# Decode attention behind a full DMA stream: an uneven load of wq, transposes of 32 keys, and V as the stationary operand in the last two tiles

## The chip, the cores and the metric

The kernel runs on one core of a Trainium2 chip. The metric is the device time of one execution in microseconds. Every run listed here is fast, so all comparisons are fast against fast. A run's time is about 1.7 to 2.0 us longer than the span of its profile (for example 1288.89 us against 1287.1 us in the profiled execution of the kernel before). Times inside a run, such as "1282.67 us", are counted from the start of the span.

## The reference

One decode step: layer norm, attention of one query per head over a cache of 8192 keys, a SwiGLU block beside it, and the residual.

```python
# B=4, D=512, H=32, Sk=8192, Dh=128, F=1792, everything bfloat16
xn = layernorm(x)
q  = (xn @ wq).reshape(B, 1, H, Dh).transpose(0, 2, 1, 3)
p  = softmax(einsum("bhqd,bhkd->bhqk", q, k_cache) * Dh ** -0.5)
o  = einsum("bhqk,bhkd->bhqd", p, v_cache).transpose(0, 2, 1, 3).reshape(B, 1, H * Dh)
out = x + o @ wo + (silu(xn @ w_gate) * (xn @ w_up)) @ w_down
```

K and V are 256 MiB each; with the weights 550.77 MB have to be read.

## The kernel before

The cache is cut into 64 tiles of two heads and one batch, 4 MB of K and 4 MB of V each. SP (SyncE) issues all the large loads in program order; a pool of five 4 MB slots holds K tiles, V tiles and weights. VectorE transposes K in SBUF, 16 keys per partition at a time, PE multiplies, and two tiles share one softmax. V is two tiles behind K (`LP = 2`).

```python
NT, T, TG, NTG, NV, LP = 64, 128, 16, 8, 4, 2      # tiles, rows per partition, rows per piece, pieces ...

wq_t = slot()                                       # one transfer, 128 partitions x 32 KB
nc.sync.dma_start(out=wq_t[:], in_=A_wq.rearrange("(p c) n -> p (c n)", c=EC))

def t_piece(n, g):                                  # VectorE: 16 keys per partition at once
    ...
    nc.vector.transpose(out=kt..., in_=src...)
def s_piece(n, g):                                  # PE: four score matmuls of 512 columns on that piece
    ...
def pt_turn(gr):                                    # VectorE: transposes the probabilities of two tiles into ptz
    ...
def pv_chunk(n, k):                                 # V is the moving operand: 32 matmuls of 512 columns a tile
    mm(o_acc[j % 2][...], pt[n // 2][...], v_tiles[n][:, k * 512:(k + 1) * 512], start=(k == 0))
def pv_last(xps, ts):                               # V is the stationary operand: 128 matmuls of 2 columns a tile
    ...
def fin_1(j):                                       # o_acc -> SBUF and a sum over its four parts
    nc.scalar.copy(out=o_sb..., in_=o_acc[j % 2][:])            # ScalarE
    nc.vector.tensor_tensor(out=o_sb[:], in0=o_sb[:], ...)      # VectorE, waits for the copy
    nc.vector.reduce_sum(out=o1[:], in_=o_sb...)                # VectorE

for i in range(NT + LP):
    # load_k(i + 2); load_v(i), the last two V tiles in 4 and 5 pieces; weights of the FFN, wo (at i = 57)
    if i < NT:
        for g in range(NTG):
            t_piece(i, g); s_piece(i, g)
            if g == 0 and bb == 0 and gr > 0: pt_turn(gr - 1)
        ...
    elif i == NT:
        pt_turn(NT // 2 - 1)                        # probabilities of tiles 62 and 63
    npv = i - LP                                    # the V tile of this turn
    if npv == NT - 1:                               # tile 63
        pv_last(xps, range(T // 2)); fin_2(...); pv_last(xps, range(T // 2, T)); fin_3(...)
    elif npv >= 0:
        for k in range(NK): pv_chunk(npv, k) ...
        if bv == B - 1 or npv == NT - 2: fin_1(jv)  # after every fourth tile, and after tile 62
        ...
```

Of the kernel before, what the change touches and what calls it, by code (L numbers as in the profile page):

```python
# [8 lines left out]
dt = mybir.dt  # L9
ACT = mybir.ActivationFunctionType  # L10
ALU = mybir.AluOpType
# [4 lines left out]
def kernel(  # L16
# [13 lines left out]
    nc = tc.nc  # L30
    P = nc.NUM_PARTITIONS

    B, Sq, D = A_x.shape
    _, H, Sk, Dh = A_k_cache.shape
# [3 lines left out]
    EC = D // P  # L38
    FC = F // P
    M = B * H  # L40
    HT = 2
    NT = M // HT
    T = HT * Sk // P
    QB = 32
    NQ = P // QB
    TG = 16
    NTG = T // TG
    NV = 512 // Dh
    SLOT = T * Dh
    NSLOT = 5  # L50
# [11 lines left out]
    slots = ctx.enter_context(tc.tile_pool(name="slots", bufs=NSLOT))  # L62
    const = ctx.enter_context(tc.tile_pool(name="const", bufs=1))
    persist = ctx.enter_context(tc.tile_pool(name="persist", bufs=1))
    kt_pool = ctx.enter_context(tc.tile_pool(name="ktp", bufs=5))
    pp = ctx.enter_context(tc.tile_pool(name="pp", bufs=2))
    small = ctx.enter_context(tc.tile_pool(name="small", bufs=2))
    psS = ctx.enter_context(tc.tile_pool(name="psS", bufs=2, space=bass.MemoryType.PSUM))
# [6 lines left out]
    def mm(out_ap, lhsT, rhs, start, **kw):  # L75
        nc.tensor.matmul(out_ap, lhsT=lhsT, rhs=rhs, start=start, stop=True,  # L76
                         skip_group_check=True, **kw)

    def slot():
        return slots.tile([P, SLOT], dt.bfloat16, name="slot")  # L80
# [3 lines left out]

    x_sb = persist.tile([B, D], dt.bfloat16, name="x_sb")
    nc.scalar.dma_start(out=x_sb[:], in_=x_flat[:, :])
    wq_t = slot()
    nc.sync.dma_start(out=wq_t[:], in_=A_wq.rearrange("(p c) n -> p (c n)", c=EC))

    k_tiles, v_tiles = {}, {}  # L90

# [6 lines left out]
    def load_v(n, parts=(T,)):  # L98
        j, b = divmod(n, B)
        t_ = slot()  # L100
        src = A_v_cache[b, j * HT:(j + 1) * HT, :, :].rearrange("h (p t) d -> (h p) (t d)", t=T)
        c0 = 0
        for w in parts:
            c1 = c0 + w * Dh
            nc.sync.dma_start(out=t_[:, c0:c1], in_=src[:, c0:c1])
            c0 = c1
        v_tiles[n] = t_
# [11 lines left out]
    zq = [const.tile([P, 2, 4, ZW], dt.bfloat16, name=f"zq{i}") for i in range(2)]  # L119
    for z_ in zq:  # L120
        nc.gpsimd.memset(z_[:], 0.0)
    xnt_w = const.tile([P, EC, QB], dt.bfloat16, name="xnt_w")
    nc.gpsimd.memset(xnt_w[:], 0.0)
    o_acc = [psO.tile([P, 512], dt.float32, name=f"oacc{i}") for i in range(2)]
    for o_ in o_acc:
# [35 lines left out]
    nc.scalar.activation(out=std[:], in_=vsum[:], func=ACT.Sqrt, bias=epst[:, 0:1], scale=1.0 / D)  # L161
    rstd = persist.tile([B, 1], dt.float32, name="rstd")
    nc.vector.reciprocal(out=rstd[:], in_=std[:])
    xn_bf = kt_pool.tile([B, D], dt.bfloat16, name="kt")
    nc.vector.tensor_scalar(out=xn_bf[:], in0=xc[:], scalar1=rstd[:, 0:1], scalar2=None, op0=ALU.mult)  # L165


    xnt_ps = psX.tile([P, EC, B], dt.bfloat16, name="xps")
    for c in range(EC):
        nc.tensor.transpose(xnt_ps[:, c, :], xn_bf[0:B, c:D:EC], ident[0:B, 0:B])  # L170
    nc.vector.tensor_copy(out=xnt_w[:, :, 0:B], in_=xnt_ps[:])


    NH = H * Dh // 512 // NQ
    q_ps = [psS.tile([P, 512], dt.float32, name="sps") for _ in range(NH)]
    for c in range(EC):
        for half in range(NH):
            for cg in range(NQ):
                n0 = c * H * Dh + (half * NQ + cg) * 512
                mm(q_ps[half][cg * QB:(cg + 1) * QB, :], xnt_w[:, c, :], wq_t[:, n0:n0 + 512], start=(c == 0))  # L180

    q_bf = slots.tile([P, NH, 2, 8, NQ, QB], dt.bfloat16, name="slot")
    for half in range(NH):
        for par in range(2):
            src = q_ps[half][:].rearrange("p (x i r) -> p x i r", x=8, r=2)[:, :, :, par]
# [83 lines left out]
                out=zq[gr % 2][a * QB:(a + 1) * QB, :, :, XO + a * QB].rearrange("p b (j r) -> p r j b", r=2),  # L269
                in_=qt[a * QB:(a + 1) * QB, half, :, hh * 2:hh * 2 + 2, cg * B + bp * 2:cg * B + bp * 2 + 2])  # L270

    def t_piece(n, g):

        w = TG * Dh
        kt = kt_pool.tile([P, w], dt.bfloat16, name="kt")
        src = k_tiles[n][:, g * w:(g + 1) * w].bitcast(dt.uint32)
        nc.vector.transpose(out=kt[:].bitcast(dt.uint32).rearrange("p (j t r) -> p t j r", j=2, r=QB),  # L277
                            in_=src.rearrange("p (t j r) -> p t j r", j=2, r=QB))
        kts[n, g] = kt

    def s_piece(n, g):
        gr, bb = divmod(n, 2)
        if bb == 0 and g == 0:
            s_ps[gr] = psS.tile([P, 512], dt.float32, name="sps")
        kt = kts.pop((n, g))[:].rearrange("p (j n r) -> p j n r", j=2, r=2)
        off = XO - 2 * (bb * NTG + g)
        for jp in range(4):
            mm(s_ps[gr][:], zq[gr % 2][:, bb, jp, off:off + P], kt[:, jp // 2, :, jp % 2],
               start=(bb == 0 and g == 0 and jp == 0))
# [6 lines left out]
    def max_2(gr):  # L296

        mps = psM.tile([P, 512], dt.float32, name="mps")
        nc.tensor.matmul(mps[:, 0:P], lhsT=nmx.pop(gr)[:, 0:1].to_broadcast([P, P]), rhs=ident_f[:, :],  # L299
                         is_transpose=True, start=True, stop=True, skip_group_check=True)  # L300
        nm = small.tile([P, HT, 2], dt.float32, name="nm")
        nc.vector.tensor_reduce(out=nm[:], in_=by_row(mps[:, 0:P]), axis=AX.XY, op=ALU.max, negate=True)  # L302
        nc.vector.tensor_tensor(out=nm[:], in0=nm[:], in1=rowb_q[:], op=ALU.mult)
        nb = small.tile([P, 1], dt.float32, name="nb")
        nc.vector.reduce_sum(out=nb[:], in_=nm[:], axis=AX.XY)
        p_ = pp.tile([P, 512], dt.bfloat16, name="p_")
        rs = small.tile([P, 1], dt.float32, name="rs")
        nc.scalar.activation(out=p_[:], in_=s_ps.pop(gr)[:], func=ACT.Exp, bias=nb[:, 0:1], scale=qscale,
                             accum_out=rs[:])
        pt[gr] = p_  # L310
        rs_t[gr] = (rs, mps)
# [27 lines left out]
        mm(o_acc[j % 2][b * QB:b * QB + w, :], pt[n // 2][:, off:off + (w - 1) * QB + 1:QB],  # L339
           v_tiles[n][:, k * 512:(k + 1) * 512], start=(k == 0))  # L340

    def pv_last(xps, ts):

        n = NT - 1
        for t in ts:
            k, u = divmod(t, NV)
            off = p_off(n, k) + u * QB
            mm(xps[:, :, B - 1], v_tiles[n][:, t * Dh:(t + 1) * Dh], pt[n // 2][:, off:off + NV * QB + 1:NV * QB],
               start=(t == 0))

    def fin_1(j):
        o_sb = pp.tile([P, NV, Dh], dt.float32, name="o_sb")
        nc.scalar.copy(out=o_sb[:].rearrange("p u d -> p (u d)"), in_=o_acc[j % 2][:])  # L353
        nc.vector.tensor_tensor(out=o_sb[:], in0=o_sb[:], in1=rowu[:].unsqueeze(2).to_broadcast([P, NV, Dh]), op=ALU.mult)  # L354
        o1 = pp.tile([P, Dh], dt.float32, name="o1")
        nc.vector.reduce_sum(out=o1[:], in_=o_sb[:].rearrange("p u d -> p d u"), axis=AX.X)  # L356
        osb[j] = o1
# [4 lines left out]
    def fin_2(j, xps, nb=B, start=True):  # L362
        mm(xps[:, :, 0:nb], osb.pop(j)[:], rowy[:, :, 0:nb], start=start)
# [25 lines left out]
    for i in range(NT + LP):  # L389

        if i + 2 < NT:
            load_k(i + 2)
        nv = i + 2 - LP
        if 0 <= nv < NT:
            load_v(nv, (32, 32, 32, 16, 16) if nv == NT - 1 else (32,) * 4 if nv == NT - 2 else (T,))
        if i == R_FFN - 3:
            load_ffn()
        if i == R_FFN:
            do_ffn()
        if i == R_WO - 2:  # L400
            load_wo()
        gr, bb = divmod(i, 2)
        if i < NT:
            for g in range(NTG):
                t_piece(i, g)
                s_piece(i, g)
                if g == 0 and bb == 0 and gr > 0:
                    pt_turn(gr - 1)
            if bb == 1:
                if gr + 1 < NT // 2:  # L410
                    build_q(gr + 1)
                max_1(gr)
        elif i == NT:
            pt_turn(NT // 2 - 1)
        npv = i - LP
        if npv == NT - 1:
            xps = x_tile()
            pv_last(xps, range(T // 2))
            fin_2(H // HT - 1, xps, nb=B - 1, start=False)
            pv_last(xps, range(T // 2, T))  # L420
            fin_3(H // HT - 1, xps)
            wo_ready = H
        elif npv >= 0:
            for k in range(NK):
                pv_chunk(npv, k)
                if k == 4 and i < NT and bb == 1:
                    max_2(gr)
            jv, bv = divmod(npv, B)
            if bv % 2 == 0:
                row_sums(npv // 2)  # L430
            if bv == B - 1 or npv == NT - 2:
                fin_1(jv)
            if bv == B - 1:
                if jv < JL:
                    fin_q(jv)
                    if jv % 2 == 1:
                        wo_ready = (jv + 1) * HT
                else:
                    xps = x_tile()
                    fin_2(jv, xps)  # L440
                    fin_3(jv, xps)
                    wo_ready = (jv + 1) * HT
        elif i < NT and bb == 1:
            max_2(gr)
        if i >= R_WO:
            for _ in range(8):
                if wo_next < wo_ready:
                    wo_mm(wo_next)
                    wo_next += 1
# [40 lines left out]
```

## Time and profile before

| | |
|---|---|
| median of three runs | 1288.78 us (1288.62 to 1288.79) |
| span, mean granted TensorE clock of the profiled run | 1287.1 us, 0.933 |
| data | 550.77 MB, 428 GB/s over the span |
| the last piece of V lands | 1282.67 us |
| the last matmul on V ends | 1283.30 us |
| after it | normalisation, four matmuls with wo, two casts, output: 3.8 us |

The main lines of the page and of the tail are shown and read in the prediction below.

### The profile page before, as it was taken

The page shows a single profiled execution, that of the slowest core. Times are in us where ns is not written, and L with a number is a line of the kernel's source. Part 1 is how long each engine was busy: PE and PEld are TensorE (multiplying, and loading weights), DVE is VectorE, ACT ScalarE, POOL GpSimd, SP SyncE. Part 2 cuts the span into 40 slices and gives each one's busy share as a digit, 9 for nine tenths or more (in the row PEclk, how much of TensorE's full clock was granted, in tenths as well). Part 3 has the DMA queues.
Part 4 walks back from the last instruction along what each step waited for, and adds up shares of the span by engine and source line. Part 5 has one row for each costly group of instructions (what it writes and reads, how often), then busy time and mean ns, then how long its engine had stood idle before and what let it go on. Part 6 is the DMA issues. An engine that isn't in the chain of part 4 may idle for free.

```text
span 1287.1 us, 11189 instructions
## 1 busy us (share of the span) xinstructions
PE 1083.1 (84%) x4778; PEld 430.3 (33%) x4778; DVE 738.1 (57%) x951; ACT 39.7 (3%) x87; POOL 5.3 (0%) x13
## 2 busy tenths in 40 slices
PE   4888888888888798897997888888887988978788
PEld 1334333333333333332333333333333333333334
DVE  6663556546556556466556566465465465573544
ACT  1000000000000000000000000000000000000000
POOL 1000000000000000000000000000000000000000
PEclk9898898998989999898998989989899898989899
DMA  9999999999999999999999999999999999999997
GB/s 407 427 430 435 437 425 437 429 436 431 432 435 428 436 432 433 431 432 435 431 435 428 434 432 431 436 431 433 430 434 431 437 430 432 433 431 427 433 434 304
DMA packets 21529, 551.49 MB, mean 428 GB/s; under 512 B 2268, under 2 KB 2792, under 8 KB 3944
## 3 DMA queue, kind: packets, MB, share of 16 engines
q1 hardware_dynamic: 21464, 550.78, 99.4%
q8 instruction: 37, 0.61, 0.2%
q14 instruction: 12, 0.10, 0.0%
q10 hardware_dynamic: 16, 0.01, 0.0%
HBM read 550.77 MB, written 0.00 MB: 428 GB/s over the span
## 4 chain that ended last, share of the span: by engine, by line
DMA 50%; PE 31%; DVE 14%; issue 5%; ACT 1%; SPq 0%; DVEq 0%
DMA slot<-in_A_k_cache_dram 44%; PE oacc L76 17%; PE sps L76 12%; DVE kt L277 11%; DMA slot<-in_A_v_cache_dram 6%; PE mps L76 1%; DVE ptz L318 1%; DVE o L356 1%; PE xps L76 1%; DVE o_sb L354 1%; ACT o_sb L353 0%; PE mps L299 0%; DVE otn L377 0%; PE yo_ps L76 0%; DVE rcp L328 0%
## 5 line engine op out<-in xcount | busy, mean ns | idle before, releaser
L76 PE MATMUL sps<-kt,zq 128*128 128x512 bf16 x2048 | 578.3, 421 | 145.2 <-DVE kt L277 128.7
L277 DVE STREAM_TRANSPOSE kt<-slot 128x1024 uint32<-128x1024 uint32 x512 | 587.6, 1210 | 90.4 <-DMA slot<-in_A_k_cache_dram 89.5
L76 PE MATMUL oacc<-slot,ptz 128*8 128x512 bf16 x2016 | 450.4, 379 | 0.4 <-DMA slot<-in_A_v_cache_dram 0.4
L76 PEld LDWEIGHTS <-zq 128*128 128x128 bf16 x2048 | 212.0, 104 | 496.1 <-issue 317.0
L76 PEld LDWEIGHTS <-ptz 128*8 128x8 bf16 x2016 | 177.5, 92 | 258.1 <-issue 27.8
L328 DVE RECIPROCAL rcp<-mps 128x4 f32<-128x4 f32 x32 | 5.9, 183 | 281.9 <-PE mps L76 281.9
L354 DVE TENSOR_TENSOR o_sb<-o_sb,rowu 128x512 f32<-128x512 f32 x16 | 11.1, 693 | 89.2 <-ACT o_sb L353 89.0
L76 PE MATMUL xps<-rowy,o 128*32 128x4 f32 (+1 forms) x228 | 13.5, 205 | 37.3 <-DVE o L356 37.3
L293 DVE TENSOR_REDUCE mx<-sps 128x1 f32<-128x512 f32 x32 | 22.1, 692 | 18.5 <-PE sps L76 18.5
L76 PEld LDWEIGHTS xps<-rowy,o 128*32 128x32 f32 (+1 forms) x228 | 12.1, 154 | 44.9 <-DVE o L356 44.9
L268 DVE COPY zq<-qt 32x8 bf16<-32x8 bf16 x128 | 21.3, 166 | 1.3
L302 DVE TENSOR_REDUCE nm<-mps 128x4 f32<-128x64 f32 x32 | 7.2, 225 | 24.0 <-PE mps L299 24.0
L356 DVE TENSOR_REDUCE o<-o_sb 128x128 f32<-128x512 f32 x16 | 16.3, 1020 | 0.5
L76 PEld LDWEIGHTS mps<-rowb,rs 128*128 128x128 f32 x64 | 9.5, 186 | 13.8 <-issue 13.8
L76 PEld LDWEIGHTS <-slot 128*128 128x128 bf16 x272 | 11.7, 126 | 3.5 <-DVE slot L188 2.6
L76 PE MATMUL mps<-rowb,rs 128*128 128x4 f32 x64 | 12.3, 263 | 0.0
L353 ACT COPY o_sb<-oacc 128x512 f32<-128x512 f32 x16 | 9.4, 586 | 76.8 <-PE oacc L76 76.8
L377 DVE TENSOR_TENSOR otn<-xps,rcp 32x16 bf16<-32x16 f32 x28 | 4.8, 170 | 11.7 <-PE xps L76 10.3
L299 PE MATMUL mps<-ident_f,mx 128*128 128x128 f32 x32 | 10.3, 323 | 0.8 <-DVE mx L293 0.8
L299 PEld LDWEIGHTS mps<-ident_f,mx 128*128 128x128 f32 x32 | 4.3, 133 | 14.7 <-DVE mx L293 14.2
L170 PE MATMUL xps<-ident,kt 4*128 4x4 bf16 x4 | 0.3, 173 | 10.1 <-DVE kt L165 10.1
L76 PE MATMUL yo_ps<-slot,otn 128*4 128x256 bf16 x64 | 8.2, 281 | 0.3 <-DVE otn L366 0.3
(150 smaller groups left out, 148.5 us busy)
## 6 DMA issues: line engine op xcount, KB each, us to landing
slot<-in_A_k_cache_dram SPq DMA_DIRECT2D x64, 4096.0 KB, 39.2
slot<-in_A_v_cache_dram SPq DMA_DIRECT2D x62, 4096.0 KB, 36.8
slot<-in_A_v_cache_dram SPq DMA_DIRECT2D x7, 1024.0 KB, 22.3
slot<-in_A_wq_dram SPq DMA_DIRECT2D x1, 4096.0 KB, 12.3
slot<-in_A_wo_dram SPq DMA_DIRECT2D x1, 3584.0 KB, 40.2
slot<-in_B_w_gate_dram SPq DMA_DIRECT2D x1, 1792.0 KB, 31.9
slot<-in_B_w_up_dram SPq DMA_DIRECT2D x1, 1792.0 KB, 35.8
slot<-in_B_w_down_dram SPq DMA_DIRECT2D x1, 1792.0 KB, 30.9
```

Source lines behind the costliest of these rows:

```text
L76: nc.tensor.matmul(out_ap, lhsT=lhsT, rhs=rhs, start=start, stop=True, skip_group_check=True, **kw)
L268: nc.vector.tensor_copy(out=zq[gr % 2][a * QB:(a + 1) * QB, :, :, XO + a * QB].rearrange("p b (j r) -> p r j b", r=2), in_=qt[a * QB:(a + ...
L277: nc.vector.transpose(out=kt[:].bitcast(dt.uint32).rearrange("p (j t r) -> p t j r", j=2, r=QB), in_=src.rearrange("p (t j r) -> p t j r", ...
L293: nc.vector.reduce_max(out=mx[:], in_=s_ps[gr][:], axis=AX.X)
L299: nc.tensor.matmul(mps[:, 0:P], lhsT=nmx.pop(gr)[:, 0:1].to_broadcast([P, P]), rhs=ident_f[:, :], is_transpose=True, start=True, stop=True ...
L302: nc.vector.tensor_reduce(out=nm[:], in_=by_row(mps[:, 0:P]), axis=AX.XY, op=ALU.max, negate=True)
L318: nc.vector.transpose(out=t_[y * HP:(y + 1) * HP, :, y, :, :].rearrange("p s u x -> p s (u x)"), in_=p_[y * HP:(y + 1) * HP, :].rearrange( ...
L328: nc.vector.reciprocal(out=rcp[j][:, :, 2 * bp:2 * bp + 2], in_=mps[:, P:P + B].rearrange("p (y b) -> p y b", y=HT))
L353: nc.scalar.copy(out=o_sb[:].rearrange("p u d -> p (u d)"), in_=o_acc[j % 2][:])
L354: nc.vector.tensor_tensor(out=o_sb[:], in0=o_sb[:], in1=rowu[:].unsqueeze(2).to_broadcast([P, NV, Dh]), op=ALU.mult)
L356: nc.vector.reduce_sum(out=o1[:], in_=o_sb[:].rearrange("p u d -> p d u"), axis=AX.X)
L377: nc.vector.tensor_tensor(out=otn[q0:q1, blk * 4:blk * 4 + 4, :], in0=xps[q0:q1], in1=r_[q0:q1, y, :].unsqueeze(1).to_broadcast([QB, 4, B] ...
```

## The change

Its intent can be read from the diff. One group of the DMA engines finishes the stream later than the rest (nine of the sixteen, 5.87 to 7.84 us behind the fastest at the last piece of V in the kernel before), since it also carries the fetches of instructions (37 packets on q8 and 12 on q14). The change (1) gives eight of the engines more of wq, so that the other eight start K earlier (the eight are called the lower ones here), (2) halves the number of transposes, for fewer instructions on VectorE and so fewer fetches, and (3) shortens PE's work at the end: tile 62 joins tile 63 in having V stationary, and the last piece of V has 8 rows instead of 16. The diff, cut to its core:

```diff
-    wq_t = slot()
-    nc.sync.dma_start(out=wq_t[:], in_=A_wq.rearrange("(p c) n -> p (c n)", c=EC))
+    wq_t, wq_u = slot(), slot()
+    nc.sync.dma_start(out=wq_t[:, 0:C1 * NQ_], in_=A_wq[0:C1 * P, :].rearrange("(p c) n -> p (c n)", c=C1))
+    for g in range(PH // QB):
+        r0 = C1 * P + g * 2 * QB
+        nc.sync.dma_start(out=wq_u[g * QB:(g + 1) * QB, 0:2 * NQ_],
+                          in_=A_wq[r0:r0 + 2 * QB, :].rearrange("(r e c) n -> e r (c n)", r=4, e=8))
...   # the projection of q reads five blocks of wq in place of four
-    kt_pool = ctx.enter_context(tc.tile_pool(name="ktp", bufs=5))
+    kt_pool = ctx.enter_context(tc.tile_pool(name="ktp", bufs=3))        # buffers of twice the size
...
-            load_v(nv, (32, 32, 32, 16, 16) if nv == NT - 1 else (32,) * 4 if nv == NT - 2 else (T,))
+            load_v(nv, (64, 32, 16, 8, 8) if nv == NT - 1 else (64, 64) if nv == NT - 2 else (T,))
...
-            for g in range(NTG):
-                t_piece(i, g)
-                s_piece(i, g)
-                if g == 0 and bb == 0 and gr > 0:
+            nd = 1 if i >= NT - 2 else ND                                # ND = 2
+            for k in range(0, NTG, nd):
+                t_piece(i, k, nd)
+                for g in range(k, k + nd):
+                    s_piece(i, g)
+                if k == 0 and bb == 0 and gr > 0:
                     pt_turn(gr - 1)
...
-        if npv == NT - 1:
+        if npv == NT - 2:
             xps = x_tile()
-            pv_last(xps, range(T // 2))
-            fin_2(H // HT - 1, xps, nb=B - 1, start=False)
-            pv_last(xps, range(T // 2, T))
+            pv_last(npv, xps, range(T), start=True)
+            row_sums(npv // 2)
+            fin_2(H // HT - 1, xps, nb=B - 2, start=False)
+        elif npv == NT - 1:
+            pv_last(npv, xps, range(T))
             fin_3(H // HT - 1, xps)
...
-            if bv == B - 1 or npv == NT - 2:
+            if bv == B - 1 or npv == NT - 3:
                 fin_1(jv)
```

Not shown above: the probabilities `p_` and the copy `o_sb` get one buffer instead of two.

More of the change, by code (lines that the diff above doesn't have):

```diff
@@ L47 @@
     NTG = T // TG
+    ND = 2
     NV = 512 // Dh
@@ L86 @@
     nc.scalar.dma_start(out=x_sb[:], in_=x_flat[:, :])
-    wq_t = slot()
-    nc.sync.dma_start(out=wq_t[:], in_=A_wq.rearrange("(p c) n -> p (c n)", c=EC))
+    NQ_ = H * Dh
+    C1, PH = EC - 1, P // 2
+    wq_t, wq_u = slot(), slot()
[4 more added lines that the diff above has]
+                          in_=A_wq[r0:r0 + 2 * QB, :].rearrange("(r e c) n -> e r (c n)", r=4, e=8))
     k_tiles, v_tiles = {}, {}
@@ L121 @@
         nc.gpsimd.memset(z_[:], 0.0)
-    xnt_w = const.tile([P, EC, QB], dt.bfloat16, name="xnt_w")
+    NX = EC + C1 + 2
+    xnt_w = const.tile([P, NX, QB], dt.bfloat16, name="xnt_w")
     nc.gpsimd.memset(xnt_w[:], 0.0)
@@ L163 @@
     nc.vector.reciprocal(out=rstd[:], in_=std[:])
-    xn_bf = kt_pool.tile([B, D], dt.bfloat16, name="kt")
-    nc.vector.tensor_scalar(out=xn_bf[:], in0=xc[:], scalar1=rstd[:, 0:1], scalar2=None, op0=ALU.mult)
-    xnt_ps = psX.tile([P, EC, B], dt.bfloat16, name="xps")
-    for c in range(EC):
-        nc.tensor.transpose(xnt_ps[:, c, :], xn_bf[0:B, c:D:EC], ident[0:B, 0:B])
-    nc.vector.tensor_copy(out=xnt_w[:, :, 0:B], in_=xnt_ps[:])
+    xn_bf = kt_pool.tile([B, D + P], dt.bfloat16, name="kt")
+    nc.vector.tensor_scalar(out=xn_bf[:, 0:D], in0=xc[:], scalar1=rstd[:, 0:1], scalar2=None, op0=ALU.mult)
+    cols = [(P, slice(c, D, EC)) for c in range(EC)]
+    cols += [(P, slice(c, C1 * P, C1)) for c in range(C1)]
+    cols += [(PH, slice(D + c * PH, D + (c + 1) * PH)) for c in range(2)]
+    for g in range(PH // QB):
+        r0 = C1 * P + g * 2 * QB
+        nc.vector.tensor_copy(
+            out=xn_bf[:, D:D + 2 * PH].rearrange("b (c g e r) -> b g c e r", c=2, g=PH // QB, e=8)[:, g],
+            in_=xn_bf[:, r0:r0 + 2 * QB].rearrange("b (r e c) -> b c e r", r=4, e=8))
+    xnt_ps = psX.tile([P, NX, B], dt.bfloat16, name="xps")
+    for c in list(range(EC, NX)) + list(range(EC)):
+        w, cs = cols[c]
+        nc.tensor.transpose(xnt_ps[0:w, c, :], xn_bf[0:B, cs], ident[0:B, 0:B])
+    nc.vector.tensor_copy(out=xnt_w[:, 0:NX - 2, 0:B], in_=xnt_ps[:, 0:NX - 2, :])
+    nc.vector.tensor_copy(out=xnt_w[0:PH, NX - 2:NX, 0:B], in_=xnt_ps[0:PH, NX - 2:NX, :])
     NH = H * Dh // 512 // NQ
     q_ps = [psS.tile([P, 512], dt.float32, name="sps") for _ in range(NH)]
-    for c in range(EC):
+    for c in range(EC, NX):
+        w = cols[c][0]
+        wt, c0 = (wq_t, c - EC) if w == P else (wq_u, c - EC - C1)
         for half in range(NH):
             for cg in range(NQ):
-                n0 = c * H * Dh + (half * NQ + cg) * 512
-                mm(q_ps[half][cg * QB:(cg + 1) * QB, :], xnt_w[:, c, :], wq_t[:, n0:n0 + 512], start=(c == 0))
-    q_bf = slots.tile([P, NH, 2, 8, NQ, QB], dt.bfloat16, name="slot")
+                n0 = c0 * NQ_ + (half * NQ + cg) * 512
+                mm(q_ps[half][cg * QB:(cg + 1) * QB, :], xnt_w[0:w, c, :], wt[0:w, n0:n0 + 512], start=(c == EC))
+    q_bf = wq_u[:, 2 * NQ_:3 * NQ_].rearrange("p (n r x c i) -> p n r x c i", n=NH, r=2, x=8, c=NQ)
     for half in range(NH):
@@ L270, in build_q, with t_piece @@
                 in_=qt[a * QB:(a + 1) * QB, half, :, hh * 2:hh * 2 + 2, cg * B + bp * 2:cg * B + bp * 2 + 2])
-    def t_piece(n, g):
+    def t_piece(n, g, nd):
         w = TG * Dh
-        kt = kt_pool.tile([P, w], dt.bfloat16, name="kt")
-        src = k_tiles[n][:, g * w:(g + 1) * w].bitcast(dt.uint32)
-        nc.vector.transpose(out=kt[:].bitcast(dt.uint32).rearrange("p (j t r) -> p t j r", j=2, r=QB),
+        kt = kt_pool.tile([P, ND * w], dt.bfloat16, name="kt")
+        src = k_tiles[n][:, g * w:(g + nd) * w].bitcast(dt.uint32)
+        nc.vector.transpose(out=kt[:, 0:nd * w].bitcast(dt.uint32).rearrange("p (j t r) -> p t j r", j=2, r=QB),
                             in_=src.rearrange("p (t j r) -> p t j r", j=2, r=QB))
-        kts[n, g] = kt
+        for i in range(nd):
+            kts[n, g + i] = kt[:, 0:nd * w].rearrange("p (j n r) -> p j n r", j=2, r=2)[:, :, i * 512:(i + 1) * 512, :]
     def s_piece(n, g):
@@ L284, in s_piece @@
             s_ps[gr] = psS.tile([P, 512], dt.float32, name="sps")
-        kt = kts.pop((n, g))[:].rearrange("p (j n r) -> p j n r", j=2, r=2)
+        kt = kts.pop((n, g))
         off = XO - 2 * (bb * NTG + g)
@@ L305, in max_2 @@
         nc.vector.reduce_sum(out=nb[:], in_=nm[:], axis=AX.XY)
-        p_ = pp.tile([P, 512], dt.bfloat16, name="p_")
+        p_ = pp.tile([P, 512], dt.bfloat16, name="p_", bufs=1)
         rs = small.tile([P, 1], dt.float32, name="rs")
@@ L340, in pv_chunk, with pv_last @@
            v_tiles[n][:, k * 512:(k + 1) * 512], start=(k == 0))
-    def pv_last(xps, ts):
-        n = NT - 1
+    def pv_last(n, xps, ts, start=False):
         for t in ts:
@@ L347, in pv_last @@
             off = p_off(n, k) + u * QB
-            mm(xps[:, :, B - 1], v_tiles[n][:, t * Dh:(t + 1) * Dh], pt[n // 2][:, off:off + NV * QB + 1:NV * QB],
-               start=(t == 0))
+            mm(xps[:, :, n % B], v_tiles[n][:, t * Dh:(t + 1) * Dh], pt[n // 2][:, off:off + NV * QB + 1:NV * QB],
+               start=start and t == ts[0])
     def fin_1(j):
-        o_sb = pp.tile([P, NV, Dh], dt.float32, name="o_sb")
+        o_sb = pp.tile([P, NV, Dh], dt.float32, name="o_sb", bufs=1)
         nc.scalar.copy(out=o_sb[:].rearrange("p u d -> p (u d)"), in_=o_acc[j % 2][:])
```

## The prediction

> **What bounds the kernel now.** I read the page first: busy shares and the DMA row, then the queue table, then the chain that ended last, then the timeline of the last 12 us, and at the end the trace's own stamps of when each DMA engine finished its share of each transfer.
>
> ```profile
> PE 1083.1 (84%) x4778; PEld 430.3 (33%) x4778; DVE 738.1 (57%) x951; ACT 39.7 (3%) x87; POOL 5.3 (0%) x13
> DMA  9999999999999999999999999999999999999997
> ...
> q1 hardware_dynamic: 21464, 550.78, 99.4%
> q8 instruction: 37, 0.61, 0.2%
> q14 instruction: 12, 0.10, 0.0%
> ```
>
> The reader sees that no compute engine is full while the 16 DMA engines are busy 90% or more in 39 of 40 slices. 550.77 MB over 1287.1 us is 428 GB/s. So every removed compute instruction is worth nothing by itself; only the moment at which the last V bytes land counts, and what stands behind it. The tail in the timeline:
>
> ```profile
> 1280.70 1.44 PEld L76 LDWEIGHTS <-slot 128*128 128x128 bf16 x48
> 1280.81 1.42 PE L76 MATMUL xps<-ptz,slot 128*128 128x2 bf16 x48
> 1282.71 0.51 PEld L76 LDWEIGHTS <-slot 128*128 128x128 bf16 x16 [0.57 <-DMA slot<-in_A_v_cache_dram]
> 1282.71 0.59 PE L76 MATMUL xps<-ptz,slot 128*128 128x2 bf16 x16 [0.48 <-DMA slot<-in_A_v_cache_dram]
> 1283.34 0.17 DVE L366 TENSOR_TENSOR otn<-xps,rcp 128x8 bf16<-128x8 f32 x1 [2.83 <-PE xps L76]
> ```
>
> PE has finished everything else at 1282.2 us, waits 0.48 us for the last piece of V, and the span ends 4.4 us after that piece. The windows of the end show that not all DMA engines work to the end:
>
> ```profile
> 1270.00:1275.00 5.00, 5.00 (x29) 2.17 (x28) 0.00 (x0) 0.00 (x0) 0.00 (x0) 1.00 1.00 418
> 1275.00:1280.00 5.00, 5.00 (x81) 3.06 (x79) 1.40 (x3) 0.59 (x1) 0.00 (x0) 1.00 0.56 236
> 1280.00:1283.00 3.00, 2.03 (x64) 1.86 (x61) 0.52 (x1) 0.00 (x0) 0.00 (x0) 0.71 0.25 101
> ```
>
> The last two columns are DMA share and GB/s: from 1275 us on, about half of the engines have run dry. The trace stamps sixteen increments on each transfer's semaphore, one per DMA engine. For the last V piece they lie at 1274.8 to 1276.0 us (seven engines) and 1280.7 to 1282.7 (nine engines): a spread of 7.8 us. For the first transfer (wq) the spread was 0.5 us. It grows in steps, and each step falls on a packet of an instruction queue: a 16 KB packet of q8 costs the engine that it meets 1.42 us, and these 37 packets go round eight engines in turn (four or five each, 5.7 to 7.1 us of delay). One ninth engine gets nine of the 8 KB packets of q14, about every 138 us, at 0.84 us each: 7.6 us of delay, plus 0.3 of initial offset. It is the one that ends last, at 1282.67; the worst of the q8 engines ends at 1282.39. The q8 packets follow PE's instruction count (one per 256), the nine q14 packets follow VectorE's (one per 128, the first at instruction 64 to 70).
>
> [...] No transfer of the kernel before shows an 8-engine case; its 128-partition transfers do carry sixteen increments. [...]
>
> **The change part by part.**
> (1) wq. Before, each engine carried 256 KB of wq. After, 3 MB spread evenly is 192 KB each, and 1 MB on engines 0 to 7 is 128 KB more: 320 KB against 192 KB. A 32 KB packet starts every 1.21 us on an engine (9.68 us for the eight of a 4 MB transfer), so engines 0 to 7 run 2 x 1.21 = 2.42 us later for the whole rest, engines 8 to 15 2.42 us earlier. q and K of tile 0 come some 2.4 us later, which is hidden: SP stays 20 to 28 us of queued transfers ahead of the fastest engine through the steady part and at least 8 us in the tail.
> (2) Transposes of 32 keys. 62 of 64 tiles need 4 instead of 8: 248 VectorE instructions fewer, and 121 semaphore waits with them. The built programs hold 1190 and 824 VectorE instructions. The block fetches then fall at 64, 192, ... 704: six instead of nine (the next at 832 is past the end). The VectorE fetch engine gets 3 x 0.84 = 2.52 us back.
> Cost: PE gets its first keys of a tile after an estimated 2.3 us[...] instead of 1.25[...]. DMA time of four tiles is 77.5 us; VectorE waited for K to land by up to 5.5 us in such a cycle (717.49 us), and where K is early PE can go on at once. So this eats slack, not time.
> (3) Last two V tiles stationary. Tile 62 takes 128 small matmuls at about 28 ns (64 took 1.81 us), 3.6 us instead of 7.1, all beside the stream: worth nothing while the last piece decides. The last piece is 8 rows instead of 16: PE's part after it falls from 0.59 to about 0.3 us. PE gets 219 instructions more, one more q8 packet, on an engine that is no longer late.
>
> Sum, if the q8 engines are 8 to 15 and VectorE's fetch engine is one of 0 to 7: VectorE's engine ends at 1282.67 + 2.42 - 2.52 = 1282.57 us; the worst q8 engine at 1282.39 - 2.42 = 1279.97; plain engines of the lower half at 1277.3. So the last bytes land 0.1 us earlier, and 0.3 us comes off the tail: 1288.78 - 0.4 = **1288.4 us**.
>
> **Rivals.**
> A. Which engine is which. The trace does not number its engines. Nine of sixteen are late, so at least one late engine lies in the lower eight whatever the numbering. For my choice: the engines that started their first wq packet first are mostly the seven early ones and VectorE's, and the change itself makes sense only so. Against: two of the eight q8 engines also started early. If q8 engines lie in the lower half, the worst of them ends at 1282.39 + 2.42 = 1284.8, 2.1 us later, less 0.3: 1290.6 us.
> B. Compute becomes the bound. PE has waits already (145.2 us ahead of the score matmuls), and two-piece transposes lengthen them[...]. With compute behind by a few us at tile 63, the end would move to 1290 to 1296. Against it: slack of several us per four tiles, and tile 62's shortening gives 3.5 us back just before the end.
> C. The balance pays fully: VectorE's fetch engine is unloaded more than I count, and the end follows the q8 engines at 1280: 1286.0 us. Against it: six fetches and the extra 64 KB are both counted from the trace and the program.
>
> **Range and chances.** About 75% for the sum above (1288.0 to 1288.8), 15% for A, 5% each for B and C. The median is 1288.4; low 1287.0 leaves room for part of C, high 1290.9 holds A. A 2% change is 26 us, which none of them makes.
>
> **What would show it.** Right: the spread of the last piece's sixteen increments shrinks to about 5 us with a single straggler; q14 shows three packets fewer, q8 38; after wq, the eight engines of the lower half are 4.8 us behind the others; PE's last group has 8 matmuls of 0.3 us in total. Wrong: several stragglers beyond 1283 us (rival A), VectorE no longer waiting for K and PE still busy with tile 61 or 62 when the last piece lands (B), or last bytes at 1280 (C).

The sum came to 1288.78 - 0.4 = 1288.4 us: the cost in (2) had been counted as zero, as slack. What is cut is the reason that was given for one premise, behind the +2.42 and -2.42 us: that the two small transfers of wq run on the same eight engines. The kernel before does not show that. The changed kernel does: eight stamps for each of the two, and tile 0's keys 4.66 us or more behind the fastest on eight engines and 0.61 us or less on the others. "0 to 7", "8 to 15", "lower" and "upper" are names for these two halves; no trace numbers the engines. The 2.3 us can be read in the changed kernel too: the transpose of 32 keys at 1195.86 us takes 2.31 us.

## More of the kernel before

One further view is needed for the result: the groups of instructions. A line holds line number, engine, operation, the shapes and the count; then busy time and the mean of one in ns; then the idle time just before the group's instructions and what ended most of it.

```profile
L76 PE MATMUL sps<-kt,zq 128*128 128x512 bf16 x2048 | 578.3, 421 | 145.2 <-DVE kt L277 128.7
L277 DVE STREAM_TRANSPOSE kt<-slot 128x1024 uint32<-128x1024 uint32 x512 | 587.6, 1210 | 90.4 <-DMA slot<-in_A_k_cache_dram 89.5
```

PE waits 128.7 us in all for transposed keys, and VectorE 89.5 us for K to land. So VectorE catches up with the stream again and again: it has slack, but not much of it.

## The result, and the profile after

The changed kernel takes **1291.06 us** (median of four runs: 1291.10, 1290.81, 1291.02, 1292.71), against 1288.78 us (four runs, 1288.62 to 1288.99) for the kernel before. The ratio is 1.002, with a 95% interval of 1.0003 to 1.0038. Ratios here and below are the mean time of one kernel's fast runs over that of the other's fast runs of the same rounds, so not quite the ratio of the medians quoted. The interval does not include 1, and 1291.06 us is 0.16 us above the predicted range.

The page of the changed kernel:

```profile
PE 1052.5 (82%) x4887; PEld 429.9 (33%) x4887; DVE 722.5 (56%) x706; ACT 39.6 (3%) x87; POOL 5.4 (0%) x13
...
DMA  9999999999999999999999999999999999999996
...
q8 instruction: 38, 0.62, 0.2%
q14 instruction: 9, 0.07, 0.0%
```

The packets of instructions are as predicted: q8 38 instead of 37, q14 9 instead of 12. The DMA row is full again up to the last slice, so the body of the kernel is still bound by the stream. The two groups of the section before have become:

```profile
L77 PE MATMUL sps<-kt,zq 128*128 128x512 bf16 x2048 | 549.8, 418 | 175.9 <-DVE kt L301 173.9
L301 DVE STREAM_TRANSPOSE kt<-slot 128x2048 uint32<-128x2048 uint32 (+1 forms) x264 | 572.6, 2218 | 58.3 <-DMA slot<-in_A_k_cache_dram 57.5
```

PE now waits 173.9 us for transposed keys instead of 128.7, and VectorE only 57.5 us for K instead of 89.5: a part of the slack has been spent, as predicted. It is not gone.

The windows of the end (length, then PE, PEld, DVE, ACT and POOL busy with counts, then granted clock, DMA share, GB/s) show the first thing that is not as predicted:

```profile
1275.00:1280.00 5.00, 2.54 (x96) 2.54 (x96) 2.36 (x4) 0.00 (x0) 0.00 (x0) 0.68 0.61 249
1280.00:1283.00 3.00, 3.00 (x91) 3.00 (x88) 0.18 (x1) 0.00 (x0) 0.00 (x0) 0.50 0.17 66
1283.00:1289.10 6.10, 3.30 (x90) 2.54 (x87) 0.58 (x2) 0.36 (x1) 0.00 (x0) 0.50 0.01 3
```

From 1275 to 1280 us PE stands still for half of the time; from 1280 to 1283 it works all the time, and it still has 3.30 us of work after 1283, when hardly any DMA engine moves anything. Before, PE worked 2.03 us of the 3 us from 1280 to 1283, and its last wait there, 0.48 us, was for V. Now V waits for PE. The timeline (start, duration, engine, line, operation, count, idle before and what ended it) says why. First the kernel before:

```profile
1267.66 1.42 DVE L318 STREAM_TRANSPOSE ptz<-p__6647 64x512 bf16<-64x512 bf16 x2 [0.91 <-ACT p__6647 L308]
...
1278.13 0.59 ACT L353 COPY o_sb<-oacc 128x512 f32<-128x512 f32 x1 [10.50 <-PE oacc L76]
1278.16 1.83 PEld L76 LDWEIGHTS <-slot 128*128 128x128 bf16 x64
1278.27 1.81 PE L76 MATMUL xps<-ptz,slot 128*128 128x2 bf16 x64
```

and the changed kernel:

```profile
1273.72 0.58 ACT L377 COPY o_sb<-oacc 128x512 f32<-128x512 f32 x1 [4.50 <-PE oacc L77]
1274.34 0.69 DVE L378 TENSOR_TENSOR o_sb<-o_sb,rowu 128x512 f32<-128x512 f32 x1 [5.99 <-ACT o_sb L377]
1275.06 1.02 DVE L380 TENSOR_REDUCE o<-o_sb 128x128 f32<-128x512 f32 x1
1275.99 1.42 DVE L343 STREAM_TRANSPOSE ptz<-p__6167 64x512 bf16<-64x512 bf16 x2
1277.46 3.55 PE L77 MATMUL xps<-ptz,slot 128*128 128x2 bf16 x128 [3.84 <-DVE ptz L343]
...
1281.73 3.55 PE L77 MATMUL xps<-ptz,slot 128*128 128x2 bf16 x128
1285.32 0.17 DVE L390 TENSOR_TENSOR otn<-xps,rcp 128x8 bf16<-128x8 f32 x1 [3.65 <-PE xps L77]
```

Before, VectorE transposed the probabilities of the last two tiles at 1267.66 us, beside PE's work on V tile 61, and the copy of `o_acc` came only at 1278.13. Now the copy and its two VectorE instructions stand ahead of that transposition in VectorE's program. The first of them idles 5.99 us until ScalarE has copied `o_acc`, which waits until PE has finished tile 61. Only then come the probabilities, at 1275.99 us, and PE stands still for **3.84 us** until they are there. After that it runs 128 and 128 matmuls without one wait for DMA and ends at 1285.28 us, 2.1 us after the last piece of V had landed.

The stamps of the DMA engines are the second half of the result. Each transfer in this table increments its semaphore sixteen times, which is read as once per engine. The DMA share fits that: in the kernel before, nine of the last piece's sixteen increments (0.56) are still to come from 1276.1 to 1280.6 us, and the share there is 0.55. For the last piece of V (us behind the fastest engine):

| kernel | fastest at | the sixteen increments behind it | last at |
|---|---|---|---|
| before | 1274.83 | 0, .18, .19, .22, .24, .61, 1.20, 5.87, 5.91, 5.92, 6.29, 7.17, 7.22, 7.26, 7.56, 7.84 | 1282.67 |
| changed | 1274.82 | 0, .03, 2.17, 2.38, 2.84, 2.88, 3.25, 3.63, 3.72, 4.61, 4.68, 4.68, 4.70, **7.42, 8.24, 8.35** | 1283.17 |

The middle has drawn together, but three engines are still late, and two of them later than any before. So the last bytes land 0.5 us later, not 0.1 us earlier.

### The profile page after: what moved, and what is told of

The parts are those of the page before. It is cut to its first block, busy times and chain, and to the rows that moved or that the text cites. A ratio compares the mean times of both kernels' runs of the same rounds, so it can differ in the third digit from the quotient of the medians.

```text
span 1289.1 us, 11046 instructions
## 1 busy us (share of the span) xinstructions
PE 1052.5 (82%) x4887; PEld 429.9 (33%) x4887; DVE 722.5 (56%) x706; ACT 39.6 (3%) x87; POOL 5.4 (0%) x13
## 4 chain that ended last, share of the span: by engine, by line
DMA 48%; PE 31%; DVE 18%; issue 3%; ACT 0%; SPq 0%; DVEq 0%; ACTq 0%
DMA slot<-in_A_k_cache_dram 48%; PE oacc L77 18%; DVE kt L301 16%; PE sps L77 10%; PE mps L77 1%; DVE ptz L343 1%; PE xps L77 1%; DVE o L380 0%; PE mps L324 0%; DVE o_sb L378 0%; ACT o_sb L377 0%; SPq L97 0%; PE yo_ps L77 0%; DVE rcp L353 0%; DVE yfx L264 0%
## 5 line engine op out<-in xcount | busy, mean ns | idle before, releaser
L77 PE MATMUL sps<-kt,zq 128*128 128x512 bf16 x2048 | 549.8, 418 | 175.9 <-DVE kt L301 173.9
L301 DVE STREAM_TRANSPOSE kt<-slot 128x2048 uint32<-128x2048 uint32 (+1 forms) x264 | 572.6, 2218 | 58.3 <-DMA slot<-in_A_k_cache_dram 57.5
L77 PE MATMUL oacc<-slot,ptz 128*8 128x512 bf16 x1984 | 444.3, 379 | 0.0
L77 PEld LDWEIGHTS <-ptz 128*8 128x8 bf16 x1984 | 174.6, 92 | 254.1 <-issue 27.4
L77 PEld LDWEIGHTS <-slot 128*128 128x128 bf16 x400 | 15.2, 120 | 7.2 <-issue 4.6
L77 PE MATMUL xps<-ptz,slot 128*128 128x2 bf16 x256 | 7.1, 166 | 3.8 <-DVE ptz L343 3.8
```

Of the source, the lines that this page charges most:

```text
L77: nc.tensor.matmul(out_ap, lhsT=lhsT, rhs=rhs, start=start, stop=True, skip_group_check=True, **kw)
L301: nc.vector.transpose(out=kt[:, 0:nd * w].bitcast(dt.uint32).rearrange("p (j t r) -> p t j r", j=2, r=QB), in_=src.rearrange("p (t j r) -> ...
```

## The experiments

Two theories stand against each other for the 2.3 us. **Order:** PE is late because VectorE's order makes it wait for the probabilities; a kernel with the order mended, and nothing else, should win back what PE is behind the stream. **Stream:** the end follows the last landing, and uneven wq made that later. They are not exclusive, so the runs take each alone and both together. The runs come from two chips, each beside its own runs of the kernel before: the order mended, both mended, wq alone and the transposes alone on one chip (nine runs before, median 1288.76 us); wq as before, the two V kernels and the ScalarE kernel on a second one (seven runs, 1289.12 us); both mended and the first half shift on the second chip later (nine runs, 1288.90 us); the last half shift on the first chip later (ten runs, 1288.97 us). Each kernel ran four to five times.

### Order mended, all else as changed

```diff
         elif i == NT:
             pt_turn(NT // 2 - 1)
+            fin_1((NT - 3) // B)
...
-            if bv == B - 1 or npv == NT - 3:
+            if bv == B - 1:
                 fin_1(jv)
```

> The changed kernel, but the last transpose of probabilities (ptz of group 31) stands ahead of the reduction of o_acc (o_sb, o1) in VectorE's order. Theory O (order): in the changed kernel VectorE stood in line behind o_sb until PE had ended tile 61, so PE waited 3.84 us for ptz and ran the last 256 small matmuls after the data were there. Then here PE goes from tile 61 to tile 62 with under 0.5 us of wait, meets the last V piece at its landing (1283.2 us), and the time falls by 1.6 to 2.0 us, to 1289.1 to 1289.5 us. Theory D (DMA skew alone sets the end): no change, 1291.0 us, because the last landing stays. Theory C (double transposes make compute late): at most 0.5 us of gain, PE still busy with tile 62 when the last piece lands.

Measured: 1289.64 us (1289.55, 1289.64, 1289.64, 1289.95, 1291.00), ratio to the kernel before 1.0008 (0.9996 to 1.0021). That is 1.42 us below the changed kernel, and 0.1 us above what was expected. Its timeline:

```profile
1269.48 1.42 DVE L343 STREAM_TRANSPOSE ptz<-p__6167 64x512 bf16<-64x512 bf16 x2 [0.91 <-ACT p__6167 L333]
...
1273.79 3.50 PE L77 MATMUL xps<-ptz,slot 128*128 128x2 bf16 x128
...
1283.45 0.37 PE L77 MATMUL xps<-ptz,slot 128*128 128x2 bf16 x8 [0.26 <-DMA slot<-in_A_v_cache_dram]
```

The probabilities are ready 6.5 us earlier, tile 62 starts without a wait, and PE again waits for the last piece, which lands at 1283.41 us. The last group is 8 matmuls in 0.37 us (0.3 had been predicted). So the order is one cause, shown by its own removal; what is left above the kernel before goes with the later landing (1283.41 against 1282.67 us).

### wq as before, the order of the change kept

The edit puts back the one transfer of wq, with its four-block projection.

```diff
-    wq_t, wq_u = slot(), slot()
-    nc.sync.dma_start(out=wq_t[:, 0:C1 * NQ_], ...)
-    for g in range(PH // QB): ...
+    wq_t = slot()
+    nc.sync.dma_start(out=wq_t[:], in_=A_wq.rearrange("(p c) n -> p (c n)", c=EC))
```

> The changed kernel with wq loaded as before, the late order of the last ptz kept. Theory: PE, not the landing, sets the end. The double transposes and the late ptz stay; tile 63's first transpose comes at about 1255.1 us instead of 1256.0 (tile 60's keys land 0.6 us earlier without the shift), so the last small matmul ends at about 1284.3 us and the time is 1289.9 to 1290.3 us. If the landing set the end, it would be that of e3_pt_first_even_wq, 1288.3 us. If the shift were worth nothing at all: 1291.0 us.

Measured: 1289.93 us (1289.73 to 1290.09), ratio 1.0007 (0.9992 to 1.0022), as expected. The timeline:

```profile
1276.37 3.55 PE L77 MATMUL xps<-ptz,slot 128*128 128x2 bf16 x128 [3.84 <-DVE ptz L324]
...
1280.63 3.56 PE L77 MATMUL xps<-ptz,slot 128*128 128x2 bf16 x128
```

The last piece lands at 1282.53 us, and PE ends at 1284.19: it is again PE that sets the end, by the same wait of 3.84 us, but all of it 1.1 us earlier than in the changed kernel. The reason is K: with the uneven wq the last bytes of tile 60's keys land at 1195.83 us, here at 1194.75, and the first transpose of tile 63 follows at 1256.04 and 1254.94 us. An uneven load therefore delays compute as well, by its late half.

### Both mended

The two edits above together.

> As e1_pt_first, and wq is loaded as before (one transfer on 16 engines). Theory: with the order mended the end follows the last landing. Without the shift the VectorE fetch engine ends at about 1280.1 (six fetches instead of nine), the worst PE-fetch engine at about 1282.4 us; against 1283.2 us with the shift. So 1288.3 to 1288.7 us, 0.6 to 0.9 us under e1_pt_first. If the shift helped the landing, this run is slower than e1_pt_first instead.

Measured: 1288.30 us (1288.28 to 1288.41), ratio 0.9996 (0.9982 to 1.0009), at the lower end of what was expected.

```profile
1282.32 0.38 PE L77 MATMUL xps<-ptz,slot 128*128 128x2 bf16 x8 [0.21 <-DMA slot<-in_A_v_cache_dram]
```

The last piece lands at 1282.28 us, and PE waits 0.21 us for it. Against the kernel with the order alone mended this is 1.34 us less (0.6 to 0.9 had been expected), the price of the uneven wq there. On the other chip beside five rounds of the kernel before:

> The kernel of e3_pt_first_even_wq once more, on the same chip as e_half_shift: 1288.3 us, some 0.45 us under the kernel before.

Measured: 1288.37 us (1288.27 to 1288.60) against 1288.90, ratio 0.9995 (0.9982 to 1.0007). Both have this version about 0.5 us below the kernel before, and both intervals include 1: a likely gain of 0.04%, not a proved one. What it comes from fits: landing 0.4 us earlier (1282.28 against 1282.67), last group 0.2 us shorter (0.38 against 0.59). But the V part with the order mended, further below, has all nine fetches and is as far under its own kernel before (0.46 us), so a gain from the three fetches saved is not shown.

### The uneven wq alone, in the kernel before

> The kernel before with the new wq layout alone. VectorE keeps its nine fetches. If its fetch engine is one of the lower eight, its last increment moves from 1282.7 by +2.42 to 1285.1 us and the time rises by 2.0 to 2.6 us to 1290.8 to 1291.4 us. If it is one of the upper eight, the worst is a PE-fetch engine of the lower eight and the rise is below 2 us. Rival (the layout is hidden): 1288.8 us.

The edit is the wq part of the diff, with its projection, and nothing else. Measured: 1291.21 us (1291.08 to 1291.71), ratio 1.0019 (1.0005 to 1.0033), as expected.

```profile
1285.51 0.59 PE L76 MATMUL xps<-ptz,slot 128*128 128x2 bf16 x16 [0.53 <-DMA slot<-in_A_v_cache_dram]
```

Here PE waits for the stream; the last piece lands at 1285.46 us, 2.8 us later than before. This run also tells the engines apart. VectorE has its nine fetches here, not six, and the last engine is now further behind: in the second of wo's two transfers it is 12.47 us behind the fastest, and two others are 10.35 and 11.06 behind. In the changed kernel, with three fetches fewer, the three late ones are 9.38, 10.18 and 10.28 us behind there. From transfer to transfer, the lag of one of the three grows in steps of about 1.0 us (the last one from 11.60 to 12.56 here, from 8.51 to 9.48 in the changed kernel): that one, 3.1 us later here, is VectorE's engine. The other two grow in steps of 1.5 to 1.7 us, so they carry PE's packets; they differ by less than 0.9 us between the two kernels. All three belong to the lower eight: in the changed kernel they are among the eight that are late right after wq.

### The transposes of 32 keys alone

> The kernel before with transposes of 32 keys alone (with its smaller pools). Theory: landing at about 1282.4 us (PE-fetch engines; VectorE's fetch engine is 2.5 us earlier), but the tiles end 1.1 to 1.6 us later on PE, as in the changed kernel (first transpose of tile 63 at 1256.0 instead of 1254.5), and the kernel before had only 0.5 us of PE wait at the end; so PE becomes late by about 1 us: 1289.3 to 1290.0 us. If the compute stays hidden: 1288.5 us.

The edit is `ND`, `t_piece`, the loop over pieces and the pools, on the kernel before. Measured: 1288.64 us (1288.26 to 1288.93), ratio 0.9998 (0.9984 to 1.0012). This **missed**: 1289.3 to 1290.0 had been expected, with PE late by the slower first piece. The first transpose of tile 63 is only 0.6 us later than before (1255.07 against 1254.45), not 1.1 to 1.6. The slower pieces are there: from the first transpose of tile 60 to that of tile 63 it takes 60.33 us instead of 59.17. But tile 60's keys land 0.5 us earlier (1194.72 against 1195.25), which the expectation had left out. The three fetches saved do appear: 9 packets on q14, and the last piece at 1282.17 us, 0.5 us earlier. PE no longer waits for it, and ends its last matmul on V at 1283.30 us, as before:

```profile
1281.49 1.81 PE L77 MATMUL xps<-ptz,slot 128*128 128x2 bf16 x64
```

So what the stream gained, the slower pieces used up. In the changed kernel the first transpose of tile 63 is 1.59 us later than before; 0.58 of it is the later landing of tile 60's keys, and from there to tile 63 the chain takes 60.18 us.

### The V part alone, and with the order mended

> The kernel before with the last two V tiles stationary alone (16-key transposes, wq on 16 engines), ptz late in VectorE's order. Theory: PE waits 3.5 to 4 us for the last ptz after tile 61, gains 3.5 us on tile 62, and so is no earlier than before: last small matmul at about 1283.7 us, never waiting for V at the end; 1289.0 to 1289.4 us. Rival (shorter tile 62 and shorter last piece simply pay): 1288.4 us.

> As e_v_only with the last ptz ahead of the reduction. Theory: PE waits for the last V piece again, which the VectorE fetch engine lands at about 1282.7 us (nine fetches); the part after it is 0.25 us shorter than before: 1288.4 to 1288.6 us.

The edits are the V blocks of the diff on the kernel before (`p_` and `o_sb` keep their one buffer), then the same with the `fin_1` move shown above. Measured: 1289.78 us (1289.72 to 1290.64), ratio 1.0008 (0.9991 to 1.0024), and 1288.66 us (1288.62 to 1288.73), ratio 0.9997 (0.9982 to 1.0012). Both are a little over what was expected (by 0.4 and 0.06 us); the kernel before was 0.34 us slower on this chip than in the rounds that the expectation started from, which covers most of the first miss and all of the second. The first has the wait again:

```profile
1275.71 3.56 PE L77 MATMUL xps<-ptz,slot 128*128 128x2 bf16 x128 [3.84 <-DVE ptz L324]
```

Neither wq nor the transposes are touched here, so the wait of 3.84 us belongs to the V part, by its order, and 1.12 us of time hang on it in this pair.

### What a fetch costs: ScalarE made to fetch

The prediction rests on instruction fetches that delay data for good. That can be tested by itself, with an engine that has nothing to do: 2304 more tiny copies on ScalarE, 72 in every second tile, in the kernel before.

```diff
+    scr = const.tile([P, 4], dt.float32, name="scr")
+    nc.vector.memset(scr[:], 0.0)
...
+        if i < NT and bb == 0:
+            for _ in range(72):
+                nc.scalar.copy(out=scr[:, 2:3], in_=scr[:, 0:1])
```

> The kernel before with 72 one-column copies on ScalarE added in every second tile (2304 instructions, in a stretch where ScalarE is idle). Theory: each 128 of them are one more 8 KB packet on the one DMA engine that fetches for ScalarE, 18 packets of 0.57 to 0.84 us; that engine ended the last piece 0.7 us behind the fastest, and now 11 to 16 us behind, so the last landing moves from 1282.7 to 1286 to 1291 us and the time rises to 1292 to 1297 us. Rival (instruction fetch is hidden, idle engines cost nothing): 1288.8 us and 18 packets more without effect.

Measured: 1292.04 us (1291.97 to 1292.49), ratio 1.0024 (1.0009 to 1.0039), at the lower end of what was expected.

```profile
q8 instruction: 37, 0.61, 0.2%
q14 instruction: 30, 0.25, 0.0%
```

Eighteen packets more on q14 (30 against 12), and one engine's stamp of the last piece goes to 1286.15 us, 8.80 us behind the fastest. The time is 2.9 us longer. Each packet delays its engine by an estimated 0.6 us: counted from the earliest stamp of the kernel before, 1274.83 us, the engine is 11.3 us late, over 18 packets of 8 KB (0.25 MB in 30). So a fetch costs the DMA engine that carries it 1.42 us for a PE packet of 16 KB, 0.84 for one of VectorE (7.6 us over nine) and about 0.6 for one of ScalarE, both of 8 KB (the first two by the steps in the stamps of the kernel before). Here work on an idle engine was not free.

### Half the shift

If the full shift of 2.42 us each way is too much for the three late engines of the lower half, half of it might be right. The order is mended in both tries. The first put 64 rows of wq on eight engines and 64 rows on partitions 0 to 63, meant for all sixteen:

```diff
-    for g in range(PH // QB): ...
+    nc.sync.dma_start(out=wq_u[0:QB, 0:2 * NQ_], in_=A_wq[r0:r0 + PH, :].rearrange("(r e c) n -> e r (c n)", r=4, e=8))
+    nc.sync.dma_start(out=wq_u[0:PH, 2 * NQ_:3 * NQ_], in_=A_wq[r0 + PH:r0 + P, :])
```

> As e1_pt_first, but only half of the moved quarter of wq goes by an 8-engine transfer (64 rows on 32 partitions); the other 64 rows go to 64 partitions by a 16-engine transfer. So the lower eight engines are 1.21 us later and the upper eight 1.21 us earlier than with an even wq, half of the change's shift. Theory: two PE-fetch engines (four packets each) are in the lower eight, the five-packet ones in the upper: the lower two end at 5.9 + 1.2 = 7.1 us after the even kernel's fastest engine (1274.9), the upper at 7.4 - 1.2 = 6.2 us; last landing at 1281.9 to 1282.2 us against 1282.3 of e3_pt_first_even_wq, so 1287.9 to 1288.4 us, 0 to 0.4 us under it. If the skew cannot be balanced this way: about midway between e1 and e3, 1289.0 us.

Measured: 1292.97 us (1292.37 to 1295.03), ratio 1.0038 (1.0024 to 1.0051): a **miss**, on the side of neither theory. The trace shows an unplanned cost at the start. The transfer to 64 partitions landed at 19.88 us, and tile 0's keys, on the fastest engine, at 25.12 us. So this run says nothing of the shift itself. The second try spreads the same 64 rows over 128 partitions, two halves of a row each:

```diff
-    nc.sync.dma_start(out=wq_u[0:PH, 2 * NQ_:3 * NQ_], in_=A_wq[r0 + PH:r0 + P, :])
+    nc.sync.dma_start(out=wq_u[:, 2 * NQ_:2 * NQ_ + NQ_ // 2],
+                      in_=A_wq[r0 + PH:r0 + P, :].rearrange("r (h n) -> (r h) n", h=2))
```

> As e_half_shift, but the other 64 rows of wq's last quarter lie as half rows on all 128 partitions instead of on 64. e_half_shift lost 3 us at once: its 16-engine transfer wrote 64 partitions only. Theory (the destination's partitions were the trouble, the half shift itself is sound): the fastest engine gets tile 0's keys 1.2 us earlier than with an even wq (about 21.0 us), the slowest 1.2 us later, the last V piece lands at 1281.9 to 1282.2 us and the time is 1287.9 to 1288.4 us, 0 to 0.4 us under the even wq with the order mended (1288.3). If extra transfers at the start cost by themselves: over 1288.8 us.

Measured: 1289.43 us (1288.19, 1288.37, 1289.43, 1289.67, 1289.67), ratio 1.0002 (0.9988 to 1.0016), against a median of 1288.97 us before (one of whose ten runs took 1299.14 us; the median does not feel it). By the median this is a miss too; the two lowest runs are inside what was expected. The same bytes now land at 14.3 us and tile 0's keys at 20.93 us on the fastest engine. In the first try, with half of the partitions, those keys came 4.2 us later (25.12 us). The rows differ as well (8 KB against 4 KB), and no run takes the two apart.

The five times lie on two levels, 1288.2 to 1288.4 and 1289.4 to 1289.7. Their distance, 1.2 to 1.4 us, is about one PE fetch (1.42 us on its engine). The durations of the q8 packets (0.88 to 0.97 us) repeat with a period of eight, and the pattern starts one place later in the changed kernel's trace than in that of the kernel before. Whether it also starts at another place in some executions of one kernel, and makes the two levels, is not shown: the one profiled execution was on the lower level. The single runs of 1291.00 us (order mended) and 1292.71 us (changed kernel) could be of the same kind. The first try has two levels too (1292.4 to 1293.0 and 1295.0), but 2 us apart, which one fetch does not cover. Half a shift has not been shown to be better than none: the version with both mended stays the best one that was run.

## Why the prediction was wrong, and where it was right

**Right.** The stream bounds the body; fetches delay their engine for good (8.80 us at the end of the ScalarE run; the first step in the kernel before, 1.71 us at 41.54 us, is still at least 1.52 at 219 us); a wq by 8-engine transfers moves the two halves apart. After wq the stamps of tile 0's keys lie in two groups of eight, 0 to 0.61 us and 4.66 to 5.34 us behind the fastest, as the 4.8 us of the prediction. That each of the two transfers runs on eight engines, which the prediction took as given, held: each has eight stamps (12.34 to 12.98 and 14.74 to 15.41 us), and the 4.8 us say that both met the same eight. Which eight of the sixteen they are by number, no run here shows; "lower" is the prediction's name for them. q8 and q14 have the packets that were counted. VectorE's engine lies in the lower half and ends at 1282.24 us (1282.57 had been worked out). The last group has 8 matmuls and takes 0.37 us when the order lets it. Nothing near a 2% change came, as was said.

**The step that failed first** is in (3): "Tile 62 takes 128 small matmuls at about 28 ns (64 took 1.81 us), 3.6 us instead of 7.1, all beside the stream: worth nothing while the last piece decides." The 3.55 us are right, and "beside the stream" is wrong. The duration was taken from the trace, but the order of the instructions that stand before it was not. The changed call of `fin_1` put two VectorE instructions that wait for PE ahead of the transposition that PE waits for. PE lost 3.84 us, came to the last tile behind the stream, and the last piece did not decide any more. Mending it gives 1.42 us back of the 2.28. Rival B foresaw PE "still busy with tile 61 or 62 when the last piece lands", but was argued away with "tile 62's shortening gives 3.5 us back just before the end": the 3.5 us saved were eaten by the 3.84 us of the wait. It was given 5%. A lower clock is seen but cost nothing that shows: the clock was 0.50 from 1280 to 1283 us, with the order mended too, and 128 small matmuls took 3.55 us there, where 64 took 1.81 us before at a clock of 1.00. (What lowers it was not tested. In the kernel before, 25 of the 27 stretches at half clock, 175 us in all, start within 7 us of an idle stretch of PE of 1.4 us or more; 46% of the span is that near to one.)

**The second** is the condition of the sum: "if the q8 engines are 8 to 15 and VectorE's fetch engine is one of 0 to 7". The second half holds. Of the first it fails for two engines: in the stamps of the changed kernel, six of the eight engines that are early after wq grow later in steps of about 1.5 us, two do not, and two of the eight late ones do. That is rival A, in part, and its sign had been seen: "two of the eight q8 engines also started early". It was sized at 1284.8 us for the last landing, with the worst engine's five packets; the two in the lower half had four each and ended at 1283.06 and 1283.17. The step counts on top of that an end that follows the landing, which it did not. By the sum's own numbers, too, wq gains nothing: with an even wq and six fetches the worst q8 engine is last, at 1282.39 us, and wq moves the last landing to 1282.57. They imply a cost of 0.2 us; with the order mended it is 1.34 us (1289.64 against 1288.30).

**The third term**, the fewer fetches and the shorter last group together, may be right in sign: -0.4 us were predicted for the whole, and the version that keeps these two and drops the rest is 0.46 and 0.53 us below the kernel before, inside the noise of its ratio. So the 2.28 us come apart as 1.42 for the order, 1.34 for wq, and -0.46 for what was meant to help. That these add up is no check, since the steps share their ends, and the shares depend on what is there already: wq alone, in the kernel before with its nine fetches, costs 2.45 us (1291.21 against 1288.76), and the order costs 1.12 us where only the V part is there.

**Not settled, but seen further.** The spread of the last piece is 8.35 us, but in the load of wo it was 10.28 in the changed kernel: behind wo the fastest engines lost some 2 us. The traces show a part of why. SP takes 13.99 us to issue the K tile behind wo in the kernel before and 15.46 us in the changed one, where most take 0.33. On the fastest engine, that tile lands 9.71 to 9.91 us after the second part of wo in the eight runs where the issue ends at least 1.9 us before the engine has finished wo. Where it ends later, the gap grows: 10.61 us (1.18 us before), 11.63 (0.17 after, the changed kernel), 12.31 (0.62 after, the order mended), 12.22 (1.00 after, ScalarE) and 14.05 (2.37 after, wq alone). So, by these thirteen traces, the fastest engines ran dry waiting for that issue. Why it takes so long was not tested. This is also why the earlier balance of the two halves cannot be read off the end alone.

## What to carry to other kernels

When a call moves in the program, read what it puts in front of whom on the same engine, and not only how long it lasts (here VectorE idled 5.99 us in front of `o_sb` and only then took up the probabilities, 6.5 us later than with the order mended): two short instructions that wait for PE, ahead of one that PE waits for, cost more here than everything that the change set out to save. Before work is shifted between DMA engines, find out from the stamps of each transfer which of them are late, and in which half they lie; a condition left open there ("if the engines are the upper eight") is the prediction. Let each part run alone: of three parts, one was harmless, one cost 1.3 us, and one gained or lost by a line that nobody would have called a part.
